# Linear attention and two matrix products: the loads of the first stages on another queue

## The chip, the cores and the metric

The kernel runs on one core of a Trainium2 chip. A core has a matrix engine (TensorE, here PE, with its weight loads shown as PEld), a vector engine (VectorE, DVE), a scalar engine (ScalarE, ACT), a general engine (GpSimd, POOL) and a synchronizing engine (SyncE, SP). They run their own instruction lists side by side and wait for each other on semaphores. Sixteen DMA engines move data between the chip's memory (HBM) and the core's on-chip memory (SBUF); the results of PE go to eight banks of PSUM, from where DVE and ACT fetch them. A DMA is issued by POOL, which writes the descriptors in software and can convert the type on the way (queue q0), or by SP or ACT through a hardware queue (q1 and q10 here), which copies without conversion. All queues share the same sixteen DMA engines.

The metric is the time of one execution on the device in microseconds (us).

## The reference: what is computed

Inputs are r, k and v of 4 batches, 8 heads, 768 tokens and 48 channels, and w and u, one value for each head and channel. For every batch and head a 48 x 48 state runs along the tokens:

```
cur   = outer(u * k_t, v_t)
y_t   = r_t @ (state + cur)
state = w[:, None] * state + outer(k_t, v_t)
```

Then the y of all heads stand side by side as a row of 384 for each of the 3072 tokens, and two products follow: g = max(0.01 h, h) with h = y @ w_in (384 x 2048), and out = g @ w_out (2048 x 384), in float32.

## The kernel before, in words

The tokens are cut into chunks of 128, so 6 chunks for each of 4 batches give 24 **stages**; stage n is chunk n // 4 of batch n % 4 and holds 8 heads. Inside a chunk the recurrence becomes matrix products. With lnw = ln(w), two tables hold w to powers of the token's place in the chunk: qtab for r, ktab for k (lines 314 to 316). A stage then goes through these steps; the letters are those of the list ORDER, a number behind a letter is the stage:

- **k, r, v**: its loads. Stage 0's k and r come as float32 into k_f and r_f by a hardware queue (line 209, EXACT = 1), all others by POOL, converted to bf16 (line 216).
- **P** (line 350, DVE): r times qtab (Pq) and k times ktab (Pk) into the tile qk.
- **T** (line 400, PE) and **t** (line 414, ACT or DVE): Pq and Pk of stages 0 to 7 are turned by multiplying with the identity, four matmuls each, and copied to the tile tp. From stage 8 on a transposing DMA does it (X8T, line 356).
- **A** (line 424, PE) the products of all token pairs, **M** (line 438, DVE) their masking, in two halves a and b.
- **X** (line 366, DVE), **D** (line 455, PE), **Q** (line 371, DVE): the term with u, for stages 0 to 7 by way of wu = w * u as a column. For stages 8 and up the sums q (line 380, DVE) read u_tab, and POOL spreads them on a diagonal.
- **K** (line 466, PE) and **S** (line 525, DVE): the state that is carried to stage n + 4.
- **Y** (line 539, PE) and **y** (line 577, ACT): the output of the attention.
- **G** and **g** (lines 596 and 611): a quarter of the first product for one stage (12 matmuls), its leaky maximum by ACT; **J** and **j** the same for two stages. **H** and **h** (lines 645 and 658): the second product and its way to HBM by SP.
- **wi0** to **wi3** and **wo0** to **wo3**: POOL's loads of the quarters of w_in and w_out.
- **F**: so many matmuls of ones by ones (line 256) whose result nobody reads.

The order of the work is written out by hand for about the first twelve stages: ORDER (lines 27 to 38) lists the steps, and each engine, SP and POOL too, runs its own steps in the order of the list. A step waits for the tiles it reads (class Sched, lines 45 to 125), so a step that waits holds up all later ones of its engine. The list of loads carries no waits of its own: SP, ACT and POOL issue their first loads as fast as they can. Behind the list a loop (line 705) works the later stages in pairs, their loads paced by the loop's matmuls.

Before the stages come small preparations. w arrives as two half rows, PE spreads them over all partitions by multiplying with a column of ones (spread_w, line 293), ACT takes the logarithm from PSUM (log_w, line 306) and makes both tables. u arrives as one row, is converted by ACT, spread by PE and copied by ACT to u_tab (lines 325 to 337). w and u by heads (w8, u8) give the columns with wu and the decay of the state (Cm, Wl, C, W).

Of the kernel before, what the change touches and what calls it, by code (L numbers as in the profile page):

```python
# [17 lines left out]
HD = H * D  # L18
# [4 lines left out]
NSL = HD // 128  # L23

FIRST, NB, PACE = 6, B, 3
TURNED, DIAG, CARRY, EXACT = 8, 8, 4, 1
ORDER = """
w k0 r0 w8 u8 u wlz tcol k1 ones table one exps qk0 r1 v0z r5 F12 bc wi2 lnw id qtab wu8 v0 id8 u16 F13 Cm P0q ktab U
k3 P1q T0q Wl P0k utab T1q r3 P1k t0q T0k C P5q W T1k t1q@ k4 T5q t0k t1k@ tri t5q F2 A0 X0 v1 X1 F2 A1 M0a F3 D0 wi1
M0b F5 D1 F1 K0 k5 P3k P3q F11 T3k Q0 r4 F3 T3q P4k t3k F3 Y0 M1b v3 t3q T4k M1a y0 F2 K1 A3 r2 t4k Q1 F1 G0.2 M3a wi3  # L30
F1 Y1 S1 g0.2 G0.1 M3b v5 y1 X3 F2 G1.2 r7 P5k g0.1 S0 T5k g1.2 D3 P4q k6 G1.1 Q3 t5k T4q r6 g1.1 K3 P2q Y3 S3 t4q T2q
k2 X5 y3 F2 A5 X4 F1 A4 t2q M5a G3.2 v4 M4b F1 G3.3 wi0 g3.2 M4a D4 D5 G0.3 g3.3 k7 M5b G1.3 P7q g0.3 v7 Q5 K5 P6k G3.1
g1.3 S5 wo2 T6k g3.1 Y5 P6q v2 P2k t6k T6q Q4 y5 r10 F2 K4 T2k t6q@ T7q t2k Y4 v6 t7q@ A6 y4 S4 F1 A2 wo3 G1.0 M6a r11
F1 J2.7 P7k g1.0 M6b wo0 J2.0 j2.7 M2b J2.6 v8 j2.0 X2 M2a J2.2 j2.6 wo1 K7 J2.1 j2.2 v9 S7 K2 J2.4 j2.1 S2 r9 G0.0
P10q j2.4 r8 K6 J2.3 g0.0 S6 v11 D2 G3.0 j2.3 X6 Q2 k8 T7k g3.0 D6 J2.5 Q6 t7k k11 Y2 P11q j2.5 X7 A7 k9 y2 Y6 M7a k10
D7 M7b y6 G2.1 Q7 v10 G2.0 g2.1 G2.3 g2.0 G2.2 g2.3 H1 g2.2 P9q P8q H2 h1 P8k q8 X8T K8 H0 h2 P9k Q8 S8 X9T P10k P11k
K9 X10T H3 h0 q9 X11T S9 Q9 Y7 h3 A9 y7 A8 M8a M9a M9b M8b k12 r12 v12 k13 r13 v13
"""


# [4 lines left out]
class Sched:  # L45
# [7 lines left out]

    def add(self, eng, emit, R=(), W=(), dma=None):
        o = Op()
        o.eng, o.emit, o.dma, o.inc, o.val = eng, emit, dma, False, None
        deps = []
        for key in R:
            w = self.writer.get(key)
            if w is not None:  # L60
                deps.append((w, True))
        for key in W:
            w = self.writer.get(key)
            if w is not None:
                deps.append((w, False))
            for r in self.readers.get(key, ()):
                deps.append((r, False))
        o.deps = []
        for d, raw in deps:
            if d.dma is None and d.eng == eng and dma is None and (eng == "pe" or not raw):  # L70
                continue
            if d is not o and d not in o.deps:
                o.deps.append(d)
        for key in R:
            self.readers.setdefault(key, []).append(o)
        for key in W:
# [51 lines left out]
def bass_rwkv5_eagle__then__act_leaky_relu_kernel(  # L128
# [13 lines left out]
    def SB(name, shape, dt=BF16):  # L142
        return ctx.enter_context(nc.sbuf_tensor(name, shape, dt))
# [4 lines left out]
    r_sb = SB("r_sb", [128, NST, HD])  # L148
    k_sb = SB("k_sb", [128, NST, HD])
    v_sb = SB("v_sb", [128, NST, H * E])  # L150
    w_row = SB("w_row", [128, HD // 2], FP32)
    u_row = SB("u_row", [1, HD], FP32)
    one_row = SB("one_row", [128, 128], FP32)
    u_row16 = SB("u_row16", [1, HD])
    w_head = SB("w_head", [H, D], FP32)
    u_head = SB("u_head", [H, D], FP32)
    wu_head = SB("wu_head", [H, D], FP32)
# [41 lines left out]
    def give(key):  # L199
        free.append(key[1])  # L200

    def dram(h, offset, pattern):
        return bass.AP(tensor=h.tensor, offset=h.offset + offset, ap=pattern)

    def at_of(n):
        c, b = divmod(n, NB)
        return b, c * L

    def load_first(n, which):
        b, t0 = at_of(n)  # L210
        src = {"k": k, "r": r}[which][b].rearrange("h t d -> t h d")[t0:t0 + L, :, :]
        dst = {"k": k_f, "r": r_f}[which][:, n, :].rearrange("p (h d) -> p h d", d=D)
        eng, queue = {"k": ("act", A), "r": ("sp", SP)}[which]
        add(eng, lambda: queue.dma_start(dst, src), W=[(which, n)], dma=f"{which}{n}")

    def load_one(n, which, pace=()):
# [4 lines left out]
        else:  # L221
            dst = {"k": k_sb, "r": r_sb}[which][:, n, :].rearrange("p (h d) -> p h d", d=D)
        add("pool", lambda: G.dma_start(dst, src), R=pace, W=[(which, n)], dma=f"{which}{n}")  # L223

# [12 lines left out]
        add("pool", lambda: G.dma_start(w_out_sb[:, 4 * i:4 * i + 4, :], wout_view[:, 4 * i:4 * i + 4, :]),  # L237
            W=[("wout", i)], dma=f"wout{i}")

    def row(h):  # L240
        return dram(h, 0, [[HD, 1], [1, HD]])

    def by_head(h):
        return dram(h, 0, [[D, H], [1, D]])
# [11 lines left out]
    def fill(n):  # L256
# [6 lines left out]

        add("pe", emit, R=["ones"], W=[("ps", i), f"fill{n}"])

    def identity():
        add("pool", lambda: G.affine_select(ident[:, :], ones[:, 0:128], pattern=[[1, 128]], compare_op=ALU.is_equal,
                                            fill=0.0, base=0, channel_multiplier=-1), R=["ones"], W=["ident"])

# [21 lines left out]
    w_bank = []

    def spread_w():
        for half in range(2):
            w_bank.append(take())
        assert w_bank[1][1][1] == w_bank[0][1][1] + 1

        def emit():
            for half in range(2):
                at0 = slice(64 * half, 64 * half + 1)  # L300
                last = PE.matmul(w_bank[half][0][:, 0:192], one_row[at0, :], w_row[at0, :], start=True, stop=True)
            return last

        add("pe", emit, R=["one_row", "w_row"], W=[w_bank[0][1], w_bank[1][1]])

    def log_w():
        i = w_bank[0][1][1]
        add("act", lambda: A.activation(lnw[:, :].rearrange("p (two c) -> p two c", two=2),
                                        ps_all[:, i:i + 2, 0:192], AF.Ln),
            R=[w_bank[0][1], w_bank[1][1]], W=["lnw"])  # L310
        give(w_bank[0][1])
        give(w_bank[1][1])
# [12 lines left out]
    def u_cast():
        add("act", lambda: A.activation(u_row16[:, :], u_row[:, :], AF.Copy), R=["u_row"], W=["u_row16"])

    def u_spread():
        ps_u, key = u_bank["u"] = take()
        add("pe", lambda: PE.matmul(ps_u[:, 0:HD], ones[0:1, 0:128], u_row16[:, :], start=True, stop=True),  # L330
            R=["ones", "u_row16"], W=[key])

    def u_table():
        ps_u, key = u_bank["u"]
        add("act", lambda: A.activation(u_tab[:, :], ps_u[:, 0:HD], AF.Copy), R=[key], W=["u_tab"])
        give(key)

    u_bank, c_bank = {}, {}
# [319 lines left out]
    def g2_out(n, c0=0, c1=HD):  # L658
# [9 lines left out]

    half_of = {"q": 0, "k": 1, "a": 0, "b": 1}
    single = {  # L670
        "w": lambda: add("sp", lambda: SP.dma_start(
            w_row[0:65:64, :], dram(w, 0, [[HD // 2, 2], [1, HD // 2]])),
            W=["w_row"], dma="w"),
        "w8": lambda: add("sp", lambda: SP.dma_start(w_head[:, :], by_head(w)), W=["w_head"], dma="w8"),
        "u8": lambda: add("sp", lambda: SP.dma_start(u_head[:, :], by_head(u)), W=["u_head"], dma="u8"),
        "u": lambda: add("sp", lambda: SP.dma_start(u_row[:, :], row(u)), W=["u_row"], dma="u"),
        "one": lambda: add("dve", lambda: V.memset(one_row[:, :], 1.0), W=["one_row"]),
        "tcol": tokens, "ones": filled, "exps": exponents, "v0z": zero_v, "qk0": zero_qk, "wlz": zero_w,
        "id": identity, "tri": triangle, "table": preload, "id8": small_identity, "wu8": wu_product,
        "bc": spread_w, "lnw": log_w, "qtab": lambda: table(qtab, qexp, "q"), "ktab": lambda: table(ktab, kexp, "k"),  # L680
        "Cm": columns_mm, "Wl": log_columns, "C": decay_columns, "W": decay_table,
        "u16": u_cast, "U": u_spread, "utab": u_table,
    }
    stage = {
        "P": lambda n, x: prep_half(n, half_of[x]), "T": lambda n, x: turn_mm(n, half_of[x]),
# [108 lines left out]
```

## Time and profile before

| what | value |
|---|---|
| time, median of 3 runs | 171.66 us (170.48 to 172.57) |
| profiled execution: span from first to last instruction | 168.6 us; the page gives no other time for it |
| PE busy | 163.7 us, 97% |
| DVE busy | 106.9 us, 63% |
| POOL busy | 103.6 us, 61% |
| ACT busy | 90.8 us, 54% |
| granted PE clock | 1.000 |
| q0 (POOL's loads) | 76512 packets, 10.03 MB |
| q1 (SP's queue) | 21574 packets, 9.12 MB |
| q10 (ACT's queue) | 1040 packets, 0.20 MB |

A page of the profile lists the busy time of each engine, then the span in 40 slices (a digit is the busy share in tenths, 9 stands for 90% or more), the DMA queues, the chain of work that ended last, and the costliest groups of instructions. A group's row reads: line, engine, operation, the tile written and the tiles read, shapes, count, busy time and mean duration in ns, and the idle time of the engine before them with what ended it. A row of the timeline or of the chain reads: start, duration, what. A row of a queue in a window reads: packets, MB, and the time that its packets took as a share of 16 engines' time; packets of one engine overlap, so the shares can add up to more than 100%.

### The profile page before, as it was taken

The numbers are of one execution on the slowest core, as the hardware profiler recorded it, in microseconds if no ns is written. First come the engines' busy times: TensorE is split into PE (matmuls) and PEld (weight loads), VectorE is DVE, ScalarE is ACT, GpSimd is POOL, SyncE is SP. The second block draws the span as 40 slices with busy tenths as digits, with TensorE's granted clock in tenths as the row PEclk, the third lists the DMA queues.
The fourth block names the chain that finished last, engine by engine and source line by source line (L and its number), as shares of the span: only waits on it lengthen the run. The fifth ranks groups of instructions, "written<-read, shape, count | busy, mean of one in ns | idle before, by whom it ended". The sixth has DMA issues, their size and how long they took to land.

```text
span 168.6 us, 5011 instructions
## 1 busy us (share of the span) xinstructions
PE 163.7 (97%) x2170; PEld 126.1 (75%) x2170; DVE 106.9 (63%) x217; ACT 90.8 (54%) x167; POOL 103.6 (61%) x117
## 2 busy tenths in 40 slices
PE   6899999999999999999999999999999999999994
PEld 4787898988667867867867867768768668668663
DVE  6599799874583999869959959969876050000000
ACT  3837866886123933933834735735637538449221
POOL 7999999990249998994993993993708100000000
PEclk9999999999999999999999999999999999999999
DMA  6999999999999959999599399299241011011012
GB/s 99 142 151 165 170 167 173 182 184 148 130 167 187 163 75 144 155 118 173 71 140 167 64 141 177 71 132 193 59 121 47 0 51 47 0 51 47 29 68 95
DMA packets 99148, 19.67 MB, mean 117 GB/s; under 512 B 92339, under 2 KB 99126, under 8 KB 99126
## 3 DMA queue, kind: packets, MB, share of 16 engines
q0 software_dynamic: 76512, 10.03, 92.1%
q1 hardware_dynamic: 21574, 9.12, 23.2%
q8 instruction: 17, 0.28, 0.7%
q10 hardware_dynamic: 1040, 0.20, 0.6%
q14 instruction: 5, 0.04, 0.1%
HBM read 20.45 MB, written 4.72 MB: 149 GB/s over the span
## 4 chain that ended last, share of the span: by engine, by line
PE 89%; POOL 5%; DMA 4%; issue 0%; ACT 0%; POOLq 0%
PE ps L652 37%; PE ps L628 31%; PE ps L605 6%; PE ps L566 6%; DMA w_in_sb<-in_moe_w_in_dram 4%; PE ps L432 4%; PE ps L473 2%; POOL k_sb L223 2%; POOL r_sb L223 2%; PE ps L407 1%; POOL v_sb L223 1%; PE ps L559 1%; PE ps L261 0%; POOL w_in_sb L233 0%; PE ps L460 0%
## 5 line engine op out<-in xcount | busy, mean ns | idle before, releaser
L652 PE MATMUL ps<-w_out_sb,gT 128*128 128x384 bf16 (+2 forms) x400 | 65.7, 320 | 0.0
L628 PE MATMUL ps<-xT,w_in_sb 128*128 128x256 bf16 x480 | 54.7, 273 | 0.0
L652 PEld LDWEIGHTS ps<-w_out_sb,gT 128*128 128x128 bf16 x400 | 37.9, 98 | 22.0
L393 POOL TENSOR_TENSOR at<-ident,s_tok 128x512 bf16<-128x512 bf16 x32 | 35.0, 1121 | 26.9 <-DVE s_tok L386 26.9
L628 PEld LDWEIGHTS ps<-xT,w_in_sb 128*128 128x128 bf16 x480 | 46.6, 98 | 6.4 <-ACT xT L580 0.2
L638 ACT ACTIVATE gT<-ps 128x512 bf16<-128x512 f32 x80 | 47.8, 597 | 6.4 <-PE ps L628 1.6
L664 ACT ACTIVATE out_sb<-ps 128x384 f32<-128x384 f32 (+2 forms) x25 | 11.9, 478 | 52.9 <-PE ps L652 52.9
L445 DVE CAST_PREDICATED at<-mask,ps 128x512 bf16<-128x512 uint16 x32 | 19.8, 684 | 18.0 <-PE ps L432 18.0
L223 POOL DMA_DIRECT2D v_sb<-in_v_dram x24 | 22.9, 955 | 0.0
L223 POOL DMA_DIRECT2D k_sb<-in_k_dram x23 | 21.5, 965 | 0.4 <-issue 0.4
L223 POOL DMA_DIRECT2D r_sb<-in_r_dram x23 | 21.2, 930 | 0.0
L353 DVE TENSOR_TENSOR qk<-r_sb,qtab 128x384 bf16<-128x384 bf16 x23 | 14.2, 617 | 3.8 <-DMA r_sb<-in_r_dram 3.8
L353 DVE TENSOR_TENSOR qk<-k_sb,ktab 128x384 bf16<-128x384 bf16 x23 | 13.0, 570 | 1.3 <-DMA k_sb<-in_k_dram 1.3
L580 ACT ACTIVATE xT<-ps 128x384 bf16<-128x384 f32 x24 | 11.0, 491 | 4.8 <-PE ps L566 4.8
L605 PE MATMUL ps<-xT,w_in_sb 128*128 128x128 bf16 x192 | 12.5, 219 | 0.4 <-DMA w_in_sb<-in_moe_w_in_dram 0.4
L615 ACT ACTIVATE gT<-ps 128x512 bf16<-128x512 f32 x16 | 9.6, 597 | 5.3 <-PE ps L605 4.9
L605 PEld LDWEIGHTS ps<-xT,w_in_sb 128*128 128x128 bf16 x192 | 11.0, 98 | 0.8 <-DMA w_in_sb<-in_moe_w_in_dram 0.5
L384 DVE TENSOR_TENSOR rku<-r_sb,ku 128x384 bf16<-128x384 bf16 x16 | 10.8, 675 | 0.6
L566 PE MATMUL ps<-at,v_sb 128*32 128x128 bf16 x384 | 10.8, 220 | 0.0
L534 DVE TENSOR_TENSOR sum_t<-ps,st 128x384 bf16<-128x384 f32 x16 | 8.8, 551 | 2.7 <-PE ps L473 2.7
L441 DVE TENSOR_TENSOR at<-ps,mask 128x512 bf16<-128x512 f32 x16 | 10.3, 681 | 0.3 <-PE ps L432 0.3
L261 PE MATMUL ps<-ones 128*128 128x128 bf16 x69 | 8.5, 257 | 1.3 <-DVE ones L251 1.3
(60 smaller groups left out, 135.1 us busy)
## 6 DMA issues: line engine op xcount, KB each, us to landing
out_dram<-out_sb SPq DMA_DIRECT2D x23, 192.0 KB, 3.6
v_sb<-in_v_dram POOLq DMA_DIRECT2D x24, 96.0 KB, 6.3
k_sb<-in_k_dram POOLq DMA_DIRECT2D x23, 96.0 KB, 6.1
r_sb<-in_r_dram POOLq DMA_DIRECT2D x23, 96.0 KB, 5.9
w_in_sb<-in_moe_w_in_dram POOLq DMA_DIRECT2D x4, 384.0 KB, 6.8
w_out_sb<-in_moe_w_out_dram POOLq DMA_DIRECT2D x4, 384.0 KB, 9.3
tp<-qk SPq DMA_TRANSPOSE x16, 2.8
k_f<-in_k_dram ACTq DMA_DIRECT2D x1, 192.0 KB, 2.7
```

What stands on the lines that cost most here:

```text
L223: add("pool", lambda: G.dma_start(dst, src), R=pace, W=[(which, n)], dma=f"{which}{n}")
L353: add("dve", lambda: V.tensor_tensor(qk[iq][:, H * half:H * half + H, 0:D], hd(src), hd(tab[:, :]), ALU.mult), R=[(name, n), "qk"[half] + ...
L384: add("dve", lambda: V.tensor_tensor(rku[i2][:, :], r_of(n), ku[i2][:, :], ALU.mult), R=[("r", n), ("ku", i2)], W=[("rku", i2)])
L393: add("pool", lambda hh=hh, s_of=s_of: G.tensor_tensor(at[ia][:, hh, :, :], ident[:, :].unsqueeze(1).to_broadcast([128, NP, 128]), s_of.un ...
L445: add("dve", lambda: V.copy_predicated(at[n % NAT][:, hh, :, :], mask[:, :].bitcast(mybir.dt.uint16).unsqueeze(1).to_broadcast([128, NP, 1 ...
L566: last = PE.matmul(ps_y[32 * q:32 * q + 32, 128 * s:128 * s + 128], a, m, start=not whole and step == 0, stop=step == len(columns[q]) - 1)
L580: add("act", lambda: A.activation(xT[m % NX][:, :, 128 * half:128 * half + 128], ps_y[:, 0:HD].rearrange("p (s t) -> p s t", t=128), AF.Copy),
L605: last = PE.matmul(ps_g[:, 128 * f:128 * f + 128], w_in_sb[:, s, 128 * fb:128 * fb + 128], xT[ix][:, s, t], start=s == 0, stop=s == NSL - 1)
L628: last = PE.matmul(ps_g[:, 256 * f:256 * f + 256], w_in_sb[:, s, 128 * fb:128 * fb + 128], xT[ix][:, s, :], start=s == 0, stop=s == NSL - 1)
L638: add("act", lambda: A.activation(gT[ig][:, 2 * j:2 * j + 2, :].rearrange("p f t -> p (f t)"), ps_g[:, :], AF.Prelu, alpha=0.01), R=[key], ...
L652: last = PE.matmul(ps_o[:, 0:c1 - c0], gT[ig][:, s, 128 * half:128 * half + 128], w_out_sb[:, s, c0:c1], start=s == 0, stop=s == NFB - 1)
L664: add("act", lambda: A.activation(out_sb[io][:, c0:c1], ps_o[:, 0:c1 - c0], AF.Copy), R=[key], W=held)
```

## The change

EXACT goes from 1 to 4: k and r of the stages 0 to 3 are loaded as float32 into k_f and r_f, all eight by SP's hardware queue (k0 went by ACT's before, and stages 1 to 3 by POOL's converting one). w is read by one transfer that writes its row of 384 into all 128 partitions, so the ones, the two half rows, the spreading matmuls and their two PSUM banks go. u is read by a converting transfer of POOL into all partitions of u_tab, so its cast, its spreading matmul and its copy go. w8 and u8 are issued by ACT. ORDER is written anew: SP's loads come as w k1 r1 k0 r0 r2 k2 r3 k3, POOL's as r5 k4 v0 k5 v1 wi3 wi0 v2 r4 wi2 wi1 v3 v5 k7 v4 r7 r6 v7 k6 wo0 wo1 wo3 wo2 and on; the first stages are worked as 1, 0, 5 and 4 beside each other, then 2 and 3; and the fillers are 57, all ahead of A0, where there were 69 through the first half of the list.

```diff
-TURNED, DIAG, CARRY, EXACT = 8, 8, 4, 1
+TURNED, DIAG, CARRY, EXACT = 8, 8, 4, 4
 ORDER = """
-w k0 r0 w8 u8 u wlz tcol k1 ones table one exps qk0 r1 v0z r5 F12 bc wi2 lnw id qtab wu8 v0 id8 u16 F13 Cm P0q ktab U
-k3 P1q T0q Wl P0k utab T1q r3 P1k t0q T0k C P5q W T1k t1q@ k4 T5q t0k t1k@ tri t5q F2 A0 X0 v1 X1 F2 A1 M0a F3 D0 wi1
...
+w ones w8 r5 id u8 k4 qk0 v0z tcol exps table lnw ktab id8 k1 wu8 v0 k5 v1 wi3 tri wi0 v2 wlz r1 r4 F23 Cm qtab P1k T1k wi2 Wl C wi1 P1q v3 W t1k@ F7
+T1q v5 k0 r0 P5q P0k P4k t1q X1 k7 P0q F17 T0k A1 t0k T4k F4 T0q v4 t0q T5q t5q t4k r7 r6 v7 M1a k6 wo0 P5k D1 wo1 K0 wo3 M1b Q1 wo2 T5k F6 A0 r2 Y1
+X0 P2q t5k y1 k2 K1 P2k M0a T2q t2q M0b T2k r3 t2k k9 D0 k3 G1.3 Q0 P3k g1.3 P3q A2 Y0 X2 M2b y0 T3k t3k G1.0 g1.0 M2a G0.3 r9 r11 D2 T3q Q2 G0.0 Y2
+g0.3 t3q K2 S1 A5 P4q X3 T4q g0.0 y2 A3 G2.0 S2 t4q M5a G2.3 M5b g2.0 M3b A4 G1.2 g2.3 X5 G0.2 M4a D3 g1.2 M3a G2.2 g2.2 Q3 g0.2 D5 G0.1 k11 Y3 y3 Q5
+K3 g0.1 G1.1 X4 Y5 D4 y5 u G3.2 P7k G3.0 M4b K4 g3.2 Q4 r8 T7k t7k v6 G3.1 S0 Y4 P7q g3.0 y4 S4 G3.3 T7q t7q k8 K7 J2.3 P6q S3 g3.1 J2.1 g1.1 S7 P6k
...
-    w_row = SB("w_row", [128, HD // 2], FP32)
-    u_row = SB("u_row", [1, HD], FP32)
-    one_row = SB("one_row", [128, 128], FP32)
-    u_row16 = SB("u_row16", [1, HD])
+    w_all = SB("w_all", [128, HD], FP32)
...
-        eng, queue = {"k": ("act", A), "r": ("sp", SP)}[which]
+        eng, queue = "sp", SP
...
+    def rows(h):
+        return dram(h, 0, [[0, 128], [1, HD]])
...
     def log_w():
...
+        add("act", lambda: A.activation(lnw[:, :], w_all[:, :], AF.Ln), R=["w_all"], W=["lnw"])
...
+    def load_u():
+        add("pool", lambda: G.dma_start(u_tab[:, :], rows(u)), W=["u_tab"], dma="u")
...
+        "w": lambda: add("sp", lambda: SP.dma_start(w_all[:, :], rows(w)), W=["w_all"], dma="w"),
+        "w8": lambda: add("act", lambda: A.dma_start(w_head[:, :], by_head(w)), W=["w_head"], dma="w8"),
+        "u8": lambda: add("act", lambda: A.dma_start(u_head[:, :], by_head(u)), W=["u_head"], dma="u8"),
+        "u": load_u,
...
-        "bc": spread_w, "lnw": log_w, "qtab": lambda: table(qtab, qexp, "q"), "ktab": lambda: table(ktab, kexp, "k"),
+        "lnw": log_w, "qtab": lambda: table(qtab, qexp, "q"), "ktab": lambda: table(ktab, kexp, "k"),
...
-        "u16": u_cast, "U": u_spread, "utab": u_table,
```

More of the change, by code (lines that the diff above doesn't have):

```diff
@@ L25 @@
 FIRST, NB, PACE = 6, B, 3
-TURNED, DIAG, CARRY, EXACT = 8, 8, 4, 1
+TURNED, DIAG, CARRY, EXACT = 8, 8, 4, 4
 ORDER = """
-w k0 r0 w8 u8 u wlz tcol k1 ones table one exps qk0 r1 v0z r5 F12 bc wi2 lnw id qtab wu8 v0 id8 u16 F13 Cm P0q ktab U
-k3 P1q T0q Wl P0k utab T1q r3 P1k t0q T0k C P5q W T1k t1q@ k4 T5q t0k t1k@ tri t5q F2 A0 X0 v1 X1 F2 A1 M0a F3 D0 wi1
[L30 to L37, printed above, removed]
+w ones w8 r5 id u8 k4 qk0 v0z tcol exps table lnw ktab id8 k1 wu8 v0 k5 v1 wi3 tri wi0 v2 wlz r1 r4 F23 Cm qtab P1k T1k wi2 Wl C wi1 P1q v3 W t1k@ F7
[3 more added lines that the diff above has]
+K3 g0.1 G1.1 X4 Y5 D4 y5 u G3.2 P7k G3.0 M4b K4 g3.2 Q4 r8 T7k t7k v6 G3.1 S0 Y4 P7q g3.0 y4 S4 G3.3 T7q t7q k8 K7 J2.3 P6q S3 g3.1 J2.1 g1.1 S7 P6k
+j2.1 v10 A7 M7b J2.4 T6q t6q r10 J2.0 j2.3 J2.5 X7 D7 j2.5 T6k t6k J2.2 Q7 k10 j2.4 J2.7 M7a X6 Y7 k13 K5 j2.2 y7 J2.6 S5 v9 P9q g3.3 A6 G2.1 v8 g2.1
+j2.0 H1 M6b P9k v13 D6 P8q q9 M6a Q9 H3 j2.6 X9T Q6 H2 K6 P8k j2.7 X8T q8 A9 M9a v11 P11q S6 Y6 y6 Q8 h2 H0 h3 K8 P10k h0 v12 P10q r13 S8 M9b P11k h1
+A8 k12 r12 K9 X10T M8b X11T M8a S9
 """
@@ L238, in load_wout @@
             W=[("wout", i)], dma=f"wout{i}")
-    def row(h):
-        return dram(h, 0, [[HD, 1], [1, HD]])
+    def rows(h):
+        return dram(h, 0, [[0, 128], [1, HD]])
     def by_head(h):
@@ L289, in zero_w @@
         add("dve", lambda: V.memset(wu[:, :, :], 0.0), W=["wu"])
[L291 to L304, printed above, removed]
-    def log_w():
[L307 to L312, printed above, removed]
+    def log_w():
+        add("act", lambda: A.activation(lnw[:, :], w_all[:, :], AF.Ln), R=["w_all"], W=["lnw"])
     def table(dst, exps, name):
@@ L323, in wu_product @@
             R=["w_head", "u_head"], W=["wu_head"])
[L325 to L338, printed above, removed]
+    def load_u():
+        add("pool", lambda: G.dma_start(u_tab[:, :], rows(u)), W=["u_tab"], dma="u")
+    c_bank = {}
     at_bank, kv_bank, y_bank = {}, {}, {}
@@ L670, in bass_rwkv5_eagle__then__act_leaky_relu_kernel @@
     single = {
[L671 to L677, printed above, removed]
+        "w": lambda: add("sp", lambda: SP.dma_start(w_all[:, :], rows(w)), W=["w_all"], dma="w"),
+        "w8": lambda: add("act", lambda: A.dma_start(w_head[:, :], by_head(w)), W=["w_head"], dma="w8"),
+        "u8": lambda: add("act", lambda: A.dma_start(u_head[:, :], by_head(u)), W=["u_head"], dma="u8"),
+        "u": load_u,
         "tcol": tokens, "ones": filled, "exps": exponents, "v0z": zero_v, "qk0": zero_qk, "wlz": zero_w,
         "id": identity, "tri": triangle, "table": preload, "id8": small_identity, "wu8": wu_product,
-        "bc": spread_w, "lnw": log_w, "qtab": lambda: table(qtab, qexp, "q"), "ktab": lambda: table(ktab, kexp, "k"),
+        "lnw": log_w, "qtab": lambda: table(qtab, qexp, "q"), "ktab": lambda: table(ktab, kexp, "k"),
         "Cm": columns_mm, "Wl": log_columns, "C": decay_columns, "W": decay_table,
-        "u16": u_cast, "U": u_spread, "utab": u_table,
     }
```

## The prediction

> **What bounds the kernel now.** The page first: the busy shares, then the slices.
>
> ```profile
> span 168.6 us, 5011 instructions
> ## 1 busy us (share of the span) xinstructions
> PE 163.7 (97%) x2170; PEld 126.1 (75%) x2170; DVE 106.9 (63%) x217; ACT 90.8 (54%) x167; POOL 103.6 (61%) x117
> ...
> DMA  6999999999999959999599399299241011011012
> ```
>
> PE is the bound, and the DMA engines are full from the second slice to the fifteenth. Busy PE may be filler (L261 multiplies ones by ones), so next the chain that ended last, in order of time:
>
> ```profile
> 9.86 6.43 DMA w_in_sb<-in_moe_w_in_dram
> 16.34 0.84 PE ps L605 x12
> 17.29 0.67 PE ps L605 x12
> 17.96 0.22 PE ps L407 x4
> ...
> 155.87 10.46 PE ps L652 x80
> 166.35 0.28 ACT out_sb L664
> ```
>
> Up to 16.34 us the chain is POOL issuing loads and one w_in load landing; from there on it is PE without a break to 166.33. So the time is **one gate plus a fixed rest**: the moment from which PE never waits again, and the matmuls that are left. What PE has done by the gate, by groups of the stretch 0 to 16.33:
>
> ```profile
> L261 PE MATMUL ps<-ones 128*128 128x128 bf16 x59 | 6.8, 263 | 1.3 <-DVE ones L251 1.3
> L407 PE MATMUL ps<-ident,qk 128*128 128x128 bf16 x32 | 3.5, 278 | 0.0
> L432 PE MATMUL ps<-tp 48*128 48x128 bf16 x24 | 1.4, 247 | 0.0
> L301 PE MATMUL ps<-w_row,one_row 1*128 1x192 f32 x4 | 1.0, 603 | 0.3 <-DMA w_row<-in_w_dram 0.3
> L605 PE MATMUL ps<-xT,w_in_sb 128*128 128x128 bf16 x12 | 0.8, 219 | 0.0
> L566 PE MATMUL ps<-at,v_sb 128*32 128x128 bf16 x32 | 0.8, 222 | 0.0
> ```
>
> 59 fillers, 8 half-stage turnings T (4 matmuls each), 3 A (8 each), one G (12), the Y of two stages (16 each); the order adds 2 K and 2 D. At the pace of the dense part (0.22 a T, 0.67 a G) that is some 5 us of useful work in 16.3. Everything else, 150 us, comes behind.
>
> **The gate after the change.** In the new order PE comes, before the turning T3k, to 9 T, 3 A, 2 D, 2 K, Y1, Y0 and one G: the same work as before the old gate plus one T. T3k reads stage 3's scaled k, and k3 is the ninth and last load on SP's queue (w k1 r1 k0 r0 r2 k2 r3 k3). What follows T3k is all the rest, so
>
> after span = 168.6 + (start of T3k - 16.34) - 0.2 (one T more done) - 0.5 (of 69 fillers 10 stand behind the old gate, 0.05 each; none behind the new) + 0.3.
>
> The last 0.3 is for the next waits of PE behind T3k: DVE needs P3q, X2, M2b, M2a, Q2 (2.8 us by the rows below) before Y2, while PE has T3k, G1.0, G0.3, D2, T3q, G0.0 (2.6); further on DVE keeps ahead. So even is T3k at 16.7, and as P3k takes 0.54 on DVE, **k3 has to land by 16.1**.
>
> **When k3 lands.** A float32 load on a hardware queue is 1024 runs of 192 bytes, 64 on each of 16 engines. Two such loads are in the trace (issue to landing):
>
> ```profile
> k_f<-in_k_dram ACTq DMA_DIRECT2D x1, 192.0 KB, 2.7
> r_f<-in_r_dram SPq DMA_DIRECT2D x1, 192.0 KB, 3.8
> ```
>
> The first ran alone, the second's end beside POOL's loads. What the queues did from 3.6 to 3.7, then from 4.2 to 4.3 (packets, MB, share of 16 engines):
>
> ```profile
> q1 hardware_dynamic: 103, 0.02, 109.6%
> q0 software_dynamic: 7, 0.00, 12.6%
> ```
>
> ```profile
> q0 software_dynamic: 131, 0.01, 236.8%
> q1 hardware_dynamic: 10, 0.00, 16.7%
> ```
>
> Alone: 103 packets in 0.1 us, so a load in 1.0 us, 17 ns a packet on its engine (1.096 x 16 x 100 / 103). Beside q0: 10 packets of 27 ns. The count is an end of r_f on a few engines only, so two readings are open: each engine still serves q1 back to back at 27 ns (1.75 us a load), or all engines together pass 100 a microsecond (10 us a load). I take 27 ns beside POOL's small packets, because 16.7% of 16 engines is 2.7 engines kept busy by q1, which fits a tail on three of them, and keep 10 us as the far end.
>
> POOL's own loads, from 10 to 12 us (k, r, v alone) and from 7.5 to 8 us (w_in nearly alone):
>
> ```profile
> q0 software_dynamic: 2917, 0.28, 264.6%
> ```
>
> ```profile
> q0 software_dynamic: 99, 0.10, 124.9%
> ```
>
> So a k, r or v load is 0.71 us of all engines (0.8 with q1 beside it); a block of w_in or w_out (384 rows, 24 on each engine) 2.0 us, 82 ns a packet. Beside those the trace has no hardware load. From below: an equal share of time, 27 ns again. From above: two weight packets to one of q1, 180 ns. I take one to one, 82 + 16 = 98 ns, since at 27 ns q1 also passes about one packet to one or two of POOL's small ones (11 ns each).
>
> The new order then gives, with POOL's issue times from its own rows:
>
> ```profile
> 1.41 1.06 POOL L223 DMA_DIRECT2D k_sb<-in_k_dram  x1 [0.38 <-issue]
> ```
>
> ```profile
> 4.20 0.78 POOL L233 DMA_DIRECT2D w_in_sb<-in_moe_w_in_dram  x1
> ```
>
> The first packets of that first load come at 3.6, 2.2 behind the issue. POOL now starts with r5 (about 0.95), id, k4, tcol, v0, k5, v1, wi3 (6.25), tri, wi0, v2, r4, wi2, wi1, then v3 v5 k7 v4 r7 r6 v7 k6 and the four wo. Data: r5 3.15 to 3.95, k4 4.55 to 5.35, v0 5.65 to 6.45, k5 6.6 to 7.4, v1 7.5 to 8.3, wi3 from 8.45, and from there POOL's data never pauses, as four weight blocks issue in 0.8 each and move in 2.0.
>
> SP: w, 196 KB, from 2.0 to 3.05 (k_f's rate). Then with 1.0 us a load in the pauses and 1.75 beside small packets: k1 done 4.4, r1 5.9, k0 7.5, and of r0 26 packets an engine are left at 8.45. wi3 and wi0 pass 50 (to 13.35): r0 done, r2 24. v2 and r4 (1.6 us at 27 ns) pass 59: r2 done, k2 18. wi2 and wi1 pass 50 (to 19.85): k2 done, r3 3. Then small packets: r3 21.5, k3 23.3, landed 23.6. T3k at 23.6 + 0.55 + 0.1 = 24.25. **Span 168.6 + 7.9 - 0.4 = 176.1.** The median of the runs, 171.66, is 3.06 above the span (the page gives the profiled execution no other time); carried over, **179.2 us**.
>
> The Trainium skill, page "DMA: Bandwidth & Descriptors", section "Queues, rings and completion order", says that an engine alternates between queues by whole packets and that one packet typically holds 9 to 17 descriptors. Against it stand the 131 and 10 above, a ratio of 13, which agrees if the 10 come from all engines; by it k3 would land with the far end, priced below.
>
> **The other edits.** w by one transfer removes four matmuls (1.0 us, L301), a memset and u's cast, spread and table; all lie before 7.2 us, while PE ran fillers. ktab is ready at about 4.5 (w landed 3.35, Ln 0.49, Exp 0.61), ahead of k1's product: nothing is gained or lost at the gate. w8 and u8 go to ACT's queue and land before 4: Cm is early, nothing waits. u by POOL, one issue of some 0.9 us, stands behind k11; only the row sums of stages 8 and up read it, behind 40 us: zero. wi3 lands near 12, before its G: zero. DVE reads six more sources in float32:
>
> ```profile
> 5.71 0.54 DVE L353 TENSOR_TENSOR qk<-r_f,qtab 128x384 bf16<-128x384 f32 x1
> ...
> 7.40 0.35 DVE L353 TENSOR_TENSOR qk<-k_sb,ktab 128x384 bf16<-128x384 bf16 x1
> ...
> 8.44 1.29 DVE L419 CAST tp<-ps 128x512 bf16<-128x512 f32 x2
> 9.64 0.75 DVE L368 TENSOR_TENSOR prod<-tp 128x512 bf16<-128x512 bf16 x2
> 10.31 1.28 DVE L441 TENSOR_TENSOR at<-ps,mask 128x512 bf16<-128x512 f32 x2
> ...
> 12.35 0.55 DVE L375 TENSOR_TENSOR vs<-v_sb,ps 128x384 bf16<-128x384 bf16 x1
> ```
>
> 6 x 0.19 = 1.1 us, hidden by the wait for k3; without that wait it counts (first rival). Behind P0k, P0q, P2q, P2k and P3k on DVE are queued the masks M, the scalings Q and the carried states S of the stages already turned; behind T3k on PE everything. No output is due on SP before 40 us, so its queue blocks nothing else.
>
> **Rivals.**
>
> 1. *Not slower: the hardware loads are not held up.* If an engine serves q1 first, k3 is down at 3.05 + 8.3 + 0.3 = 11.7, and DVE's order decides: from P1k at 4.5, seven float32 P (3.8), three bf16 P (1.05), wu's two copies (about 0.35), one t (0.65), two X (0.75), four M (2.56), two Q (1.1), 10.3 in all, T3k at 14.9. Span 166.8 and 169.8 us, 170.8 with a microsecond of waits in between. It decides if k3 lands before 14.3. For it: the first reading's 2.7 engines. Against: 27 ns beside 17. Chance 0.14.
>
> 2. *An equal share also beside the weights.* 27 ns throughout: r0 9.15, four loads of 1.75, k3 landed 16.5, T3k 17.1: 172.0; with a slowest engine a microsecond or two late, as r_f's tail was, 174. Chance 0.25, a third of it within 1%.
>
> 3. *Starved.* 100 packets a microsecond while POOL's data flow: by 8.45 some 1.4 us of pauses and 4 us beside data pass 1800 of 8320 packets; POOL's remaining 24 loads and 8 blocks flow to 43.7 and let 3500 through; the last 3000 need 3 us: k3 47, T3k 47.7, 203 us. Chance 0.12.
>
> 4. *A cold PE on top.* Fillers ran at half pace at the start and at full pace later:
>
> ```profile
> 1.34 1.46 PE L261 MATMUL ps<-ones 128*128 128x128 bf16 x12 [1.34 <-DVE ones L251]
> ```
>
> ```profile
> 11.59 0.78 PE L261 MATMUL ps<-ones 128*128 128x128 bf16 x11
> ```
>
> 0.11 us against 0.056 each. If PE, waiting most of 5 to 24 us, starts the rest at half pace, the fillers' phase (slow still at 5.6, fast by 11) bounds the loss at 0 to 3 us; I put 0 in the sum and the 3 in the range. The Trainium skill, "TensorE: Matmul & The Clock Gate", Part 1, gives a window of 3.4 us idle for half clock and as long busy for full; by it an estimate is 1.7 us more, 180.9. No row of before shows a pause that long.
>
> **Chances.** The forecast with one to one beside weights, 176 to 184, 0.45; rival 1 0.14; rival 2 0.25; starved 0.12; other mishaps of the order (slower) 0.04. A difference of 1%, 1.7 us, is about what a measurement of this kernel tells from none. Faster by over 1%: 0.05 (rival 1 without waits, nearly all of it). Within 1%: 0.09 + 0.08 = 0.17. Slower: 0.78. The range reaches down to rival 1's 170.8 and up to 188, two weight packets to one (k3 near 27.5: 183) with the 3 us of a cold PE and a late engine on top; starved lies outside.
>
> **What would show it.** The k_f and r_f issues of SP with times to landing growing down the queue, k3's over 15 us from its issue near 5; DVE's L353 waiting for r_f and k_f; the chain that ended last beginning with those DMAs; PE dense only from about 24 us and as long from there as now, 150 us; L407 on PE with idle ahead of it. Wrong it would be if k3 lands before 16, or if PE stands behind T3k again for another load.

## The result and the profile after

The changed kernel takes 185.52 us (median of 4 runs, 184.31 to 186.15) against 171.82 us (median of 4 runs, 170.48 to 172.57): **1.082 times as long**, interval 1.074 to 1.089. The forecast was 179.2 us with a range of 170.8 to 188.0. The profiled execution took 184.31 us, its span 182.6.

The page of the changed kernel (span; busy engines; PE and its granted clock in 40 slices of 4.6 us; median time from issue to landing):

```profile
span 182.6 us, 4979 instructions
...
PE 166.5 (91%) x2153; PEld 128.3 (70%) x2153; DVE 106.8 (58%) x213; ACT 90.9 (50%) x168; POOL 99.0 (54%) x112
...
PE   6574348999999999999999999999999999999994
...
PEclk9999655899999999999999999999999999999999
...
k_f<-in_k_dram SPq DMA_DIRECT2D x4, 192.0 KB, 10.0
```

PE is busy for 2.8 us more than before, with 17 matmuls fewer. It was at 97% of the span before; now it is at 3 to 8 tenths in the first seven slices, and from there as dense as before. The clock row is new as well: 5 to 8 tenths in slices five to eight. k_f, which alone took 2.7 us from issue to landing, takes 10.0 in the median. The start of the kernel, from the chain that ended last, in order of time:

```profile
9.54 3.52 SPq L209
...
13.11 14.54 DMA k_f<-in_k_dram
...
27.67 0.57 DVE qk L318
...
28.28 0.61 PE ps L372 x4
28.89 2.56 PE ps L570 x24
```

This is the gate that was forecast: stage 3's k, the last load on SP's queue, then P3k (L318 is the new line of P), then the turning T3k (L372). k3 lands at 27.65 instead of the 23.6 forecast, and T3k starts at 28.28 instead of 24.25. The chain before it is SP's own issuing. The G behind it (L570, 24 matmuls in 2.56 us) runs at half the pace of the dense part. DVE's waits name the loads (total, times, longest):

```profile
DVE qk L318 <- DMA k_f<-in_k_dram: 8.9, 3, 4.7
```

The account: by the forecast's formula the span is 168.6 + (28.28 - 16.34) - 0.4 = 180.1. Measured are 182.6, so **2.5 us are left over** beside the gate. By stretches (busy us of PE, PEld, DVE, ACT, POOL; then the granted clock, the DMA share and GB/s):

```profile
15.00:20.00 5.00, 0.67 (x8) 0.34 (x8) 0.56 (x1) 1.09 (x2) 5.00 (x7) 0.98 1.48 155
20.00:25.00 5.00, 3.51 (x47) 2.66 (x47) 2.22 (x4) 1.24 (x3) 5.00 (x7) 0.50 1.33 176
...
30.00:35.00 5.00, 5.00 (x77) 4.42 (x75) 2.61 (x7) 2.92 (x6) 5.00 (x7) 0.66 1.87 180
```

PE had 0.67 us of work from 15 to 20; after that its clock is at half. It is back to full here:

```profile
33.00:33.50 0.50, 0.50 (x6) 0.32 (x3) 0.20 (x1) 0.20 (x1) 0.50 (x2) 0.55 1.63 192
33.50:34.00 0.50, 0.50 (x21) 0.38 (x20) 0.00 (x0) 0.42 (x2) 0.50 (x2) 1.00 1.36 198
```

That is 5.2 us after PE became dense at 28.28. At half clock 5.2 us do the work of 2.6; so a cold PE could be the rest, and the first experiment asks for it.

Why k3 came so late is seen in what the queues did. Four windows of one microsecond, 13 to 14, 18 to 19, 23 to 24 and 29 to 30, and last the whole stretch from 13 to 28 (packets, MB, share of 16 engines):

```profile
q0 software_dynamic: 168, 0.15, 92.2%
q1 hardware_dynamic: 172, 0.03, 29.4%
...
q0 software_dynamic: 447, 0.05, 81.1%
q1 hardware_dynamic: 443, 0.08, 78.2%
...
q0 software_dynamic: 168, 0.16, 93.3%
...
q0 software_dynamic: 1488, 0.14, 266.3%
...
q1 hardware_dynamic: 3704, 0.70, 42.7%
```

Alone, POOL's queue passes 1488 small packets a microsecond. Beside SP's queue it passes 447, and SP's 443: **as many packets of the one as of the other**, and when POOL's are rows of weights (0.15 MB in 168 packets) SP's are held to their number too. From 12 to 25 us the two counts agree within a few per cent in each microsecond. From 5 to 12 most of them do not: POOL's queue passed 501 to 1040 in each, SP's 186 to 629, and SP's was not always the smaller. Why is open; the trace doesn't split the packets by engine.

POOL's own small packets are thinned as well, to a third; its rows of weights by less (99 in half a microsecond before, 168 in a whole one now). Its four w_in quarters (issue times, then time to landing):

```profile
L228 POOL DMA_DIRECT2D w_in_sb<-in_moe_w_in_dram x4: 748/772/786, 6.4 to 10.9; - x4
...
DMA to landing us min/median/max: 9.6/14.0/17.6
```

So the last, issued at 10.9, took the 17.6 and landed near 28.5. Before, the median was 6.8 us.

### The profile page after: what moved, and what is told of

It reads as the page before. It is cut to its first block, busy times and chain, and to the rows that moved or that the text cites. A ratio compares the mean times of both kernels' runs of the same rounds, so it can differ in the third digit from the quotient of the medians.

```text
span 182.6 us, 4979 instructions
## 1 busy us (share of the span) xinstructions
PE 166.5 (91%) x2153; PEld 128.3 (70%) x2153; DVE 106.8 (58%) x213; ACT 90.9 (50%) x168; POOL 99.0 (54%) x112
## 4 chain that ended last, share of the span: by engine, by line
PE 83%; DMA 8%; SPq 7%; DVE 0%; issue 0%; ACT 0%
PE ps L617 34%; PE ps L593 29%; DMA k_f<-in_k_dram 8%; PE ps L570 7%; SPq L209 6%; PE ps L531 5%; PE ps L397 3%; PE ps L438 2%; PE ps L372 1%; PE ps L524 1%; PE ps L425 0%; DVE qk L318 0%; SPq L636 0%; ACT out_sb L629 0%
## 5 line engine op out<-in xcount | busy, mean ns | idle before, releaser
L593 PEld LDWEIGHTS ps<-xT,w_in_sb 128*128 128x128 bf16 x480 | 46.6, 98 | 6.3
L603 ACT ACTIVATE gT<-ps 128x512 bf16<-128x512 f32 x80 | 47.5, 598 | 5.2 <-PE ps L593 0.8
L629 ACT ACTIVATE out_sb<-ps 128x384 f32<-128x384 f32 (+2 forms) x25 | 11.7, 478 | 45.7 <-PE ps L617 45.7
L218 POOL DMA_DIRECT2D v_sb<-in_v_dram x24 | 21.8, 912 | 2.0 <-issue 2.0
L218 POOL DMA_DIRECT2D r_sb<-in_r_dram x20 | 18.1, 915 | 1.6 <-issue 0.8
L218 POOL DMA_DIRECT2D k_sb<-in_k_dram x20 | 18.5, 925 | 0.0
L372 PE MATMUL ps<-ident,qk 128*128 128x128 bf16 x64 | 7.2, 248 | 12.0 <-DVE qk L318 11.8
L386 ACT ACTIVATE tp<-ps 128x512 bf16<-128x512 f32 x15 | 8.6, 598 | 15.5 <-PE ps L372 15.5
L570 PE MATMUL ps<-xT,w_in_sb 128*128 128x128 bf16 x192 | 15.1, 243 | 0.0
L372 PEld LDWEIGHTS ps<-ident,qk 128*128 128x128 bf16 x64 | 4.5, 109 | 13.4 <-DVE qk L318 13.0
L570 PEld LDWEIGHTS ps<-xT,w_in_sb 128*128 128x128 bf16 x192 | 13.3, 110 | 0.4
L318 DVE TENSOR_TENSOR qk<-r_sb,qtab 128x384 bf16<-128x384 bf16 x20 | 12.7, 633 | 1.1 <-DMA r_sb<-in_r_dram 1.0
L318 DVE TENSOR_TENSOR qk<-k_sb,ktab 128x384 bf16<-128x384 bf16 x20 | 12.8, 641 | 0.0
L580 ACT ACTIVATE gT<-ps 128x512 bf16<-128x512 f32 x16 | 9.3, 596 | 6.2 <-PE ps L570 6.1
```

The lines of the kernel that those rows point to most:

```text
L318: add("dve", lambda: V.tensor_tensor(qk[iq][:, H * half:H * half + H, 0:D], hd(src), hd(tab[:, :]), ALU.mult), R=[(name, n), "qk"[half] + ...
L372: last = PE.matmul(ps_t[:, 128 * p:128 * p + 128], qk[iq][:, h0:h0 + 2, :].rearrange("p h e -> p (h e)"), ident[:, :], start=True, stop=True)
L570: last = PE.matmul(ps_g[:, 128 * f:128 * f + 128], w_in_sb[:, s, 128 * fb:128 * fb + 128], xT[ix][:, s, t], start=s == 0, stop=s == NSL - 1)
L593: last = PE.matmul(ps_g[:, 256 * f:256 * f + 256], w_in_sb[:, s, 128 * fb:128 * fb + 128], xT[ix][:, s, :], start=s == 0, stop=s == NSL - 1)
L603: add("act", lambda: A.activation(gT[ig][:, 2 * j:2 * j + 2, :].rearrange("p f t -> p (f t)"), ps_g[:, :], AF.Prelu, alpha=0.01), R=[key], ...
L629: add("act", lambda: A.activation(out_sb[io][:, c0:c1], ps_o[:, 0:c1 - c0], AF.Copy), R=[key], W=held)
```

## The experiments

### A cold PE

Fillers stand in PE's waits, so that it never idles long; nothing else changes.

```diff
-K1 P2k M0a T2q t2q M0b T2k r3 t2k
+K1 P2k M0a F36 T2q t2q M0b F54 T2k r3 t2k
...
-y0 T3k t3k G1.0
+y0 F54 T3k t3k G1.0
```

> The changed kernel with 144 more fillers on PE: 36 ahead of T2q, 54 ahead of T2k and 54 ahead of T3k, where PE stands for 2.3, 3.4 and 3.4 us. Nothing else moves. Theory A (the gate is T3k at 28.3 us, and on top PE is at half clock when it starts the rest, granted clock 0.5 from 20.3 to 33.9 us): T3k stays at 28.3, the granted clock stays 1.0, the span falls from 182.6 by the half-clock work behind the gate, some 2.5 us, to 180.1. Rival B (the clock does not matter, the missing microseconds behind the gate are waits for DVE): the span stays at 182.6 or rises by the overshoot of the fillers.

Measured: 182.51 us (182.38 to 183.91), 1.068 times before, interval 1.062 to 1.073; 171.47 for before beside it. The granted clock is 1.00 in each stretch of 5 us between 15 and 30. From the chain of this kernel:

```profile
13.41 14.72 DMA k_f<-in_k_dram
...
28.77 0.40 PE ps L372 x4
29.17 1.34 PE ps L570 x24
```

T3k starts half a microsecond later than in the changed kernel, and yet the span is 180.6, two shorter. The same 24 matmuls take 1.34 us instead of 2.56. The formula gives 168.6 + 12.43 - 0.4 = 180.6, which is the span measured. So the rest of 2.5 us was the clock.

### POOL's weights wait for k3

The loads of SP are listed first, and POOL's third w_in quarter, the first to be issued, waits until k3 is down; all of POOL's later loads stand behind it.

```diff
-w ones w8 r5 id u8 k4 ...
+w k1 r1 k0 r0 r2 k2 r3 k3 ones w8 r5 id u8 k4 ...
...
+            R=[("k", 3)] if g == 3 else [], W=[("win", g)], dma=f"win{g}")
```

> The changed kernel, but POOL issues wi3 and all its later loads only when k3 has landed; SP's loads are named first in the order, in the same sequence. Theory A (k3 is late because the hardware queue's packets take turns one to one with those of POOL's queue): without POOL's traffic from about 9 us on, r0, r2, k2, r3 and k3 move at about 1000 packets a microsecond and k3 lands near 14 to 15 us in place of 27.6; then wi3, asked for only now, lands near 19 and sets T3k (one G with wi3 stands before it) at about 19.5; span about 171 to 174, some 10 us less, although every later load of POOL is issued some 8 us later. Rival B (the loads' own transfer, 192-byte runs, is slow on the hardware queue, or SP issues them slowly, whatever POOL does): k3 stays near 25 us or later and the kernel grows slower, 190 us or more, as w_in comes later still.

Measured: 178.42 us (178.15 to 178.76), ratio 1.042, 1.038 to 1.046. From its chain and its waits:

```profile
12.02 4.27 DMA k_f<-in_k_dram
...
25.05 0.33 PE ps L372 x4
```

```profile
DVE at L406 <- POOL mask L266: 5.6, 1, 5.6
```

k3 lands at 16.3 instead of 27.65 (14 to 15 was expected), with nothing changed but that POOL's later loads are absent until then. So POOL's traffic holds k3. The span falls by 5.7 us and not by 10. One possible reason is a cost of the edit itself: POOL makes the mask behind the load that now waits, and DVE waited 5.6 us for it. The next run takes that wait away.

### The same, with the mask made before the wait

```diff
-... wi3 tri wi0 ...
+... tri wi3 wi0 ...
```

> As the run in which POOL waits for k3 (178.4 us), but POOL makes the mask before it waits: in that run DVE's first masking stood for 5.6 us for the mask, which POOL made only behind wi3. Theory A (k3's landing was late for POOL's traffic, and the rest of that run's loss was my mask): k3 lands at 16.3 again, the masks start near 12 us, and the gate is now wi3, asked for at 16.3 and landing near 20; T3k near 21 in place of 25.0, so 174 to 176 us. Rival B (it was not the mask but the late w_in that bounded it): no change, 178.

Measured: 179.28 us (178.88 to 180.2), ratio 1.044, 1.038 to 1.050 (before: 171.54). The chain:

```profile
11.56 4.78 DMA k_f<-in_k_dram
...
16.63 4.85 DMA w_in_sb<-in_moe_w_in_dram
...
21.53 1.46 PE ps L570 x12
...
24.51 0.54 PE ps L372 x4
25.05 1.96 PE ps L570 x24
```

The wait for the mask is gone and nothing is won: now the first G waits for its quarter of w_in, which could only start at 16.6 and lands at 21.5. So the mask did not set the time of the run before either. Holding POOL back frees k3 and makes the weights the gate. The expected gain (174 to 176 us) did not come, and the rival, that the late w_in bounds it, holds. In these two runs the queue that goes second brings the gate.

### The hardware loads on two queues

k1, k0 and k2 are issued by ACT on its own queue, the other six loads by SP.

```diff
-        eng, queue = "sp", SP
+        eng, queue = ("act", A) if which == "k" and n < 3 else ("sp", SP)
```

> The changed kernel with k1, k0 and k2 on ACT's hardware queue, and w r1 r0 r2 r3 k3 on SP's. Theory A (turns are taken by queue, one packet each, so two hardware queues get two turns in three): k2 lands near 13, r2 near 16 to 17, k3 near 23.5 to 24 us in place of 27.6; the span falls by about 4 us to 178.5. Rival B (POOL's queue takes a fixed half, both hardware queues share the other): k3 stays near 27.6 and the span near 182.6. Rival C (ACT is held up by issuing into a full queue): ln(w) starts later than 4.7 us and the first P later than 6.0.

Measured: 175.92 us (175.74 to 176.98), ratio 1.029, 1.023 to 1.035. Its queues from 10 to 11 us, a wait, and its chain:

```profile
q1 hardware_dynamic: 354, 0.07, 61.1%
q0 software_dynamic: 351, 0.03, 60.8%
q10 hardware_dynamic: 350, 0.07, 32.9%
```

```profile
ACT L249 <- issue: 5.3, 1, 5.3
```

```profile
4.63 11.65 DMA k_sb<-in_k_dram
...
22.34 0.33 PE ps L372 x4
22.67 1.34 PE ps L570 x24
```

Where all three queues are busy they pass equal counts, one to one to one. Two thirds of the packets are then hardware loads instead of half, and k3 lands at 16.2, far earlier than the 23.5 to 24 that was expected from the turns alone: POOL's small loads are slowed so much that its rows of weights begin only when the hardware loads are through (q1 passes nothing from 16 us on, and q0 moves 0.21 MB in 208 packets from 17 to 18). T3k starts 6 us earlier. POOL's loads pay: k4 lands at 16.3 and begins the chain. And the third theory holds too: ACT's own issuing keeps its first activation waiting until 5.3 us (1.7 in the changed kernel), so that the first P came at 7.93 instead of 6.02. The time is nearly 10 us better than the changed kernel's, still 3% above that of before.

### Only the queue, in the old order

The kernel before, with k and r of stages 0 to 3 in float32 on SP's queue; the order, w and u stay as they were.

```diff
-TURNED, DIAG, CARRY, EXACT = 8, 8, 4, 1
+TURNED, DIAG, CARRY, EXACT = 8, 8, 4, 4
...
-        eng, queue = {"k": ("act", A), "r": ("sp", SP)}[which]
+        eng, queue = "sp", SP
```

> The kernel before with one part of the change alone: k and r of stages 0 to 3 as float32 by SP's queue (SP's sequence is then w k0 r0 w8 u8 u k1 r1 k3 r3 r2 k2), everything else and the written order as before; POOL's queue loses six loads. Theory A (turns one to one): r1 lands near 9 in place of 6.6 us and holds up DVE and PE in their order, w_in's second quarter, which set the old gate at 16.3, lands near 18; the time rises by 2 to 3 us. Rival B (the new written order is what costs, the queue does no harm): no difference, or up to 1.5 us less because POOL's loads of w_in are issued earlier.

Measured: 179.48 us (178.9 to 180.23), ratio 1.048, 1.044 to 1.053. Its chain and one of its waits:

```profile
4.54 9.20 DMA r_f<-in_r_dram
13.83 0.57 DVE qk L353
...
19.87 1.17 PE ps L261 x11
```

```profile
DVE wu_head L322 <- DMA u_head<-in_u_dram: 5.4, 1, 5.4
```

The direction was right, the size far off: 8 us and not 2 to 3. r1, only the fourth large load on the queue, takes 9.2 us and lands at 13.7. Since the old order is written for an early r1, its fillers (L261) now stand behind the wait and are paid for. Also the tiny u_head (1.5 KB), issued behind k0 and r0, keeps DVE waiting for 5.4 us, where it was 1.6 before with only r0 ahead of it: a small load inherits the delay of the queue it stands in. So the new order is not what makes the queue dear; in the old order the queue alone costs 8 us.

### Only w and u, in the old order

w into all partitions by one transfer, u by POOL, w8 and u8 on ACT's queue; the loads and the order of before.

```diff
-            w_row[0:65:64, :], dram(w, 0, [[HD // 2, 2], [1, HD // 2]])),
+            w_all[:, :], rows(w)), W=["w_all"], dma="w"),
```

> The kernel before with the other half of the change alone: w by one transfer into all partitions on SP's queue ahead of r0, w8 and u8 by ACT, u by POOL's converting transfer behind k11; the spreading matmuls, casts and copies go. The written order is otherwise that of before. Theory A (all of this lies off the gate): r0 lands some 1 us later behind the 192 KB of w, P0q starts near 6.4 in place of 5.7, the old gate (w_in's quarter at 16.3) takes most of it up: 0 to 0.8 us more, inside 0.5%. Rival B (spreading w by DMA is a cost or a gain of its own): more than 1.5 us either way.

Measured: 173.57 us (median of 12, 172.49 to 173.93), ratio 1.011, 1.008 to 1.014. One of its waits:

```profile
DVE wu_head L297 <- DMA u_head<-in_u_dram: 2.6, 1, 2.6
```

About 2 us, where 0 to 0.8 was expected: a miss, and the rival (more than 1.5) holds. What may account for it: w8 and u8 stand behind k0 on ACT's queue here, and w is 192 KB of traffic where it was 1.5; the first P comes at 7.00 instead of 5.71. In the changed kernel w8 and u8 come first on ACT's queue, and its DVE had u_head by 4.04 (the product with w_head starts there), so that part of the price should not carry over. No run takes the parts one by one.

### Only the order

The changed kernel, but k and r of stages 1 to 3 come by POOL ahead of w_in; only k0 and r0 are left on the hardware queues, k0 on ACT's and r0 on SP's, as before. POOL also makes the mask (tri) earlier.

```diff
-TURNED, DIAG, CARRY, EXACT = 8, 8, 4, 4
+TURNED, DIAG, CARRY, EXACT = 8, 8, 4, 1
...
-... id u8 k4 qk0 v0z tcol ... k5 v1 wi3 tri ...
+... id u8 k4 qk0 v0z tcol tri k1 r1 ... k5 v1 r2 k2 r3 k3 wi3 ...
```

> The changed kernel's order of PE and DVE, w and u, but k and r of stages 1 to 3 by POOL again (converted, ahead of wi3: tri k1 r1 v0 k5 v1 r2 k2 r3 k3 wi3), only k0 and r0 by the hardware queues. Theory A (the queue is the loss, not the order): k1 lands near 8.5, k3 near 16, DVE's chain to P3k takes some 10 us from k1: T3k near 19, 173 to 176 us, though POOL's loads of w_in come 5 us later than in the changed kernel. Rival B (the order is the loss): T3k not before 24 and 180 us or more.

Measured: 174.17 us (173.98 to 174.65), ratio 1.014, 1.009 to 1.020. From the chain, T3k and the G behind it:

```profile
20.40 0.33 PE ps L372 x4
20.73 1.34 PE ps L570 x24
```

The time lies in the expected 173 to 176. With the same order, and w and u as changed, the price is 2.6 us; the other 11.3 come with the loads on SP's queue, the clock's part among them. From 9.53 us this chain is nearly all PE, and 34 fillers (L256) take 3.5 us of it. What of the 2.6 is w and u, what the order and what its fillers was not taken apart.

### Two stages by two hardware queues, two by POOL

k1 and k0 on ACT's queue, r1 and r0 on SP's, r2 k2 r3 k3 by POOL ahead of w_in.

```diff
-TURNED, DIAG, CARRY, EXACT = 8, 8, 4, 4
+TURNED, DIAG, CARRY, EXACT = 8, 8, 4, 2
...
-        eng, queue = "sp", SP
+        eng, queue = ("act", A) if which == "k" else ("sp", SP)
```

> The changed kernel with EXACT = 2: k1 and k0 by ACT's hardware queue, r1 and r0 by SP's behind w, all issued first; r2 k2 r3 k3 by POOL behind v1, ahead of wi3. Theory A (what counts is that the hardware loads are few enough to be through before POOL's queue is full): k0 and r0 land near 7, k3 near 14, wi3 near 16.5, T3k at 16.5 to 17.5, so 171.5 to 172.5 us, no difference from before within 0.5%. Rival B (float32 loads on a hardware queue cost whatever their number): T3k near 20, 175 us.

Measured: 174.69 us (174.22 to 175.58), ratio 1.017, 1.013 to 1.022. The chain:

```profile
10.08 8.18 DMA w_in_sb<-in_moe_w_in_dram
...
20.42 0.54 PE ps L372 x4
20.96 2.34 PE ps L570 x24
```

A miss: 171.5 to 172.5 was expected. The gate is the first quarter of w_in, which lands at 18.3; before, a quarter that POOL issued at 9.86 was there at 16.34. The first G starts at 18.31 and T3k at 20.42, as late as in the run with the order alone, and behind it PE is at half clock besides (24 matmuls in 2.34 us). No version tried is faster than the kernel before.

## Why the prediction was right and where it was wrong

The formula of the gate can be tried on seven kernels, the changed one and the six runs that keep its order behind T3k. Each T3k is the row of the chain with L372 x4 ahead of L570 x24; the last column is that row's duration.

| kernel | T3k | span by the formula | span | difference | 24 matmuls of G |
|---|---|---|---|---|---|
| changed | 28.28 | 180.1 | 182.6 | +2.5 | 2.56 |
| cold PE filled | 28.77 | 180.6 | 180.6 | 0.0 | 1.34 |
| weights wait | 25.05 | 176.9 | 176.9 | 0.0 | 1.34 |
| the same, mask first | 24.51 | 176.4 | 177.1 | +0.7 | 1.96 |
| two hardware queues | 22.34 | 174.2 | 174.2 | 0.0 | 1.34 |
| order alone | 20.40 | 172.3 | 172.2 | -0.1 | 1.34 |
| two and two | 20.42 | 172.3 | 173.4 | +1.1 | 2.34 |

Where the G behind T3k runs at full pace the formula is right to 0.1 us. Elsewhere it falls short by about half of the time that the clock stays at half behind T3k: 5.2, 1.7 and 2.5 us in the three kernels, so 2.6, 0.9 and 1.2, against 2.5, 0.7 and 1.1. The run with fillers shows this cause for the changed kernel; for the two others it is argued. By the prediction's own steps:

- **One gate plus a fixed rest**: right. So was the gate itself: k3 as last load on SP's queue, P3k, T3k. Where the clock is full the table leaves nothing for a late DVE or for another load behind T3k.
- **Beside weight blocks one packet to one**: right. 98 ns a packet on each engine is 163 a microsecond for all; 153 to 172 were measured from 13 to 15 and from 23 to 24 us.
- **27 ns a packet beside POOL's small packets**: wrong, the term of the sum that was mis-sized. A packet's own time was right (78.2% of 16 engines for 443 packets is 28 ns). What failed is that an engine serves q1 back to back: from one packet of q1 to the next it is 36 ns, 2.3 us a load and not 1.75, with equal counts there as well. The 27 came from the tail of one load. The trace of before has a fuller window, from 4.0 to 4.1 us, where r_f was still under way:

```profile
q0 software_dynamic: 76, 0.01, 137.1%
q1 hardware_dynamic: 50, 0.01, 48.3%
```

  50 packets in 0.1 us make 2.0 us a load, and POOL's 76 are half of its own pace, so both losses could be seen there.
- **POOL's data move at their own pace**: the step that failed silently. The prediction slowed SP's loads by POOL's, and hardly POOL's by SP's (0.71 to 0.8 us a load). POOL's small packets fall to a third. At 13 us forecast and trace still agree, 3.7 loads left to pass against 3704 packets or 3.6 loads by the count from 13 to 28. That is in part luck: by the counts (3261 packets of SP's queue up to 8.45 us, w among them) 3.0 loads were through at 8.45 where the forecast had 3.6, and SP made it good because POOL's rows of weights came 2 to 3 us later than forecast. But by the forecast the w_in quarters were through at 19.85, and k3 ran from there at the pace of small packets. In the trace q0 still moves 0.16 MB in 168 packets from 23 to 24, and the last quarter lands near 28.5. Together with the line above this is the 4 us by which k3 was late; the split between the two is not measured.
- **The cold PE at 0**: wrong, 2.5 us in the trace and 2.0 net in the run with fillers. It was kept as a rival with a bound of 0 to 3, and the range held it. The Trainium skill, "TensorE: Matmul & The Clock Gate", Part 1, gives 3.4 us of work until full clock, which made an estimate of 1.7; measured were 5.2 us and 2.5. The window runs freely by the same section. The traces agree: in five kernels the half clock lasted one to four times 3.41 us (table in the last section). Counted back from 33.45, where the changed kernel is at full clock again, a window ran from 26.6 to 30.0; PE was dense from 28.28, so only the window after it was wholly busy, and the wait was 5.2 us.
- **w and u at 0**: no gain or loss at the gate in the changed kernel, where ktab came 1.5 us later than forecast (the first P at 6.02) but k3 set the end. In the old order it is 1.1%.
- **SP's issues**: the forecast had k3's near 5 us and its landing over 15 us behind that. The last four issues took 1.7 to 3.7 us each, k3's started at 13.11, and the landing came 14.5 behind it. From 12 us on that cost nothing seen, as SP's queue kept up with POOL's in each count; before 12 it is open.
- **Around the span**: 3.06 from profiled span to median, measured 2.9. Of it 1.7 belongs to each execution (184.31 against 182.6), the rest is that the profiled one was the fastest of its four runs.

The rivals: *not held up* falls, as k3 landed at 27.65 and not at 11.7. *An equal share* falls with the one-to-one counts. *Starved*: a ratio like the 13 that stood for it came back only in the tail of k3 (814 and 78 packets from 26 to 27 us), not while both queues were full. The Trainium skill, "DMA: Bandwidth & Descriptors", section "Queues, rings and completion order", has engines change queues after whole packets of typically 9 to 17 descriptors. That holds for either queue, so it gives no ratio of 13 between two full ones; the equal counts here neither bear it out nor refute it, and how many records an engine takes at a turn no run shows. *A cold PE* came true on top of the likeliest case.

The sum missed the span by 6.5 us: 4.0 for k3 and 2.5 for the clock. The measured 185.52 lies above the forecast's own band of 176 to 184. The range held it, for the clock by the right cause; for k3 that was luck, as the range's end stood for two weight packets to one (k3 near 27.5), and the counts show one to one beside the weights.

## What to carry to other kernels

A second queue on the same DMA engines is no second road: count the packets of all queues together, and expect a load to move at the pace of one packet for each of the other queue's, whatever their size, and the other queue to be slowed by it in turn. Small runs beside rows of weights fare worst: some 150 to 170 packets a microsecond, where alone there were 103 in a tenth of one. A count in the tail of a load, where few engines still work for it, is no measure of the pace. Before a late gate is priced, ask also how long PE idles ahead of it, since the clock charges for it behind the gate.

## What the runs showed of the hardware that was not expected

- Queues that are both full pass equal counts of packets whatever their size: 168 and 172, 447 and 443 in a microsecond for two queues, 354, 351 and 350 for three. A queue of small packets falls from 1488 a microsecond to 447 when a second one is busy. From 5 to 12 us of the changed kernel the counts were not equal, and why is open.
- An engine that issues hardware DMAs is held up once some loads of 1024 runs are under way. An issue of SP in the changed kernel, the third large load of k and r (start, duration; the two before it took 0.41 and 0.58):

```profile
2.35 2.23 SPq L209 DMA_DIRECT2D k_f<-in_k_dram  x1
```

  The later ones took up to 3.7. On SP this cost nothing that was seen from 12 us on; on ACT, with three loads, the first activation came 3.6 us later than in the changed kernel, and with it the logarithm and the tables.
- The granted clock follows PE's work late in both directions. In the changed kernel it came back 5.2 us after PE was dense. In the run with two stages on two queues PE stood for only 2.0 us (in brackets), is dense from 18.31, and the clock falls only behind that (a row of the timeline, then windows of that kernel):

```profile
18.31 0.84 PE L570 MATMUL ps<-xT,w_in_sb 128*128 128x128 bf16 x12 [1.99 <-DMA w_in_sb<-in_moe_w_in_dram]
```

```profile
18.00:19.00 1.00, 0.69 (x12) 0.67 (x12) 0.00 (x0) 0.00 (x0) 1.00 (x2) 1.00 2.36 149
19.00:20.00 1.00, 1.00 (x26) 0.62 (x27) 0.47 (x1) 0.60 (x1) 1.00 (x2) 0.75 1.73 191
...
23.00:24.00 1.00, 1.00 (x23) 1.00 (x22) 0.59 (x2) 0.67 (x2) 1.00 (x3) 1.00 2.27 156
```

  So an idle stretch can be paid for after the wait has ended.
- The half clock comes in whole steps of 3.41 us. From windows of 0.1 us around each change of the granted clock:

| kernel | half clock from | to | us | steps of 3.41 us |
|---|---|---|---|---|
| changed | 19.80 | 33.45 | 13.65 | 4 |
| weights wait | 13.66 | 23.90 | 10.24 | 3 |
| the same, mask first | 19.40 | 26.23 | 6.83 | 2 |
| two hardware queues | 17.97 | 21.38 | 3.41 | 1 |
| two and two | 19.50 | 22.92 | 3.42 | 1 |

  In the last of them the step ahead of the fall, from 16.09 to 19.50, had PE busy for 1.4 us of 3.41, so a step need not be wholly idle to bring the half clock.
